# The last batch's down projection by seven products of sums, with the sums of w_out formed one stage earlier

## The chip, the cores and the metric

The kernel runs on one core of a Trainium2 chip. A core has a matrix engine (PE, with its weight loads shown as PEld), three engines for element-wise work (DVE, ACT and POOL) and a queue that issues most transfers (SP). Each engine works through its own queue in order and waits on semaphores for the others. The metric is the device time of one execution in microseconds; lower is better.

## The reference, cut to what matters

The input is q, k and v of 8 batches, 8 heads, 576 positions and 64 numbers a head, and three weights: w_a and w_b of 512 x 1536 and w_out of 1536 x 512. Each position attends to itself and the 127 before it, with a bias that grows linearly with distance, by head. The heads' results stand side by side as x, of 4608 x 512, and a feed-forward layer of two branches follows:

```python
def _moe_ref(x, w_a, w_b, w_out):
    a = x @ w_a
    b = x @ w_b
    return (a * b @ w_out).astype(np.float32)
```

The inputs and the output are fp32.

## The kernel before

**Precision.** PE multiplies fp16. Every fp32 operand is kept as two fp16 tensors, the rounded value ("hi") and the rest ("lo"), and a product of two operands is three matmuls: hi x hi, hi x lo and lo x hi. So whatever is multiplied has first to be split: a copy to fp16 on ACT (`hi`), then a subtraction on DVE (`lo`). All matmuls of the feed-forward layer have 128 x 128 weights and 288 moving columns (half a batch's 576 positions, `HT`).

**Stages.** Batch 0's attention comes first, alone. Then for each batch b an *up projection* (x times w_a and w_b, and their element-wise product, the hidden layer, of 12 blocks of 128 rows, `NF`) and a *down projection* (hidden times w_out) follow one another, and the attention of batch b + 1 is spread over them in small pieces. After batch 6's down projection there is no attention left: batch 7's up projection and down projection stand alone.

**Up projection.** `up_fast` (line 858) computes one block f by seven products of sums and differences of operands in place of eight, in seven steps of six matmuls. Two blocks run in turn as two lanes (line 912). A step's result lies in a PSUM bank `ch` or `ef` and is read by ACT (lines 866, 878 and 884) or DVE (873, 889, 894 and 901). Several steps add to the bank of an earlier step: step 3 adds to the `ch` bank that line 866 must have copied first, step 5 after line 878, step 7 after line 889. POOL multiplies at line 896. `halve` (line 833) then splits the block's hidden layer into `h`. From batch 4 on all blocks go this way. The operands, sums of x, are formed by `split_x` (line 440) with POOL subtractions (lines 451 to 461), ACT copies (437) and DVE subtractions (438), during the down projection before.

**Down projection.** `down` (line 930) computes one 128 x 288 result at a time: 36 matmuls over the 12 blocks into one bank, which ACT copies out at line 942, and a transfer at line 943. Eight such results, 288 matmuls, make a batch.

**Weights.** w_out lies in `wdn` as hi and lo for all 12 blocks. `sums_of_weights` (line 233) forms the sums of w_a and w_b that `up_fast` needs, in POOL additions (246 to 250), ACT copies (255) and DVE subtractions (256), spread over batches 1 to 3.

**What sets the order.** PE's order is written out by hand (line 1023). The order of the other engines' queues is worked out by the scheduler when the kernel is built, from readiness and priority; lines under `tc.high_priority` come first among those that are ready, and `tc.issue_after` keeps an instruction behind another of its engine. `weave` (line 954) mixes side work between the steps of a stage by its place in the program; `Pace.along` (972) does the same for attention.

**Buffers.** `vhl` (two), `qkh` and `qkl` (two each), `v`, `qk`, `pT` (one each), `t` (four) and `phl` belong to attention and are free once the last batch's attention has read them. A buffer is given to its next user when its last reader is through.

Of the kernel before, what the change touches and what calls it, by code (L numbers as in the profile page):

```python
# [11 lines left out]
F32 = mybir.dt.float32  # L12
F16 = mybir.dt.float16
# [4 lines left out]
AF = mybir.ActivationFunctionType  # L18
ALU = mybir.AluOpType
AX = mybir.AxisListType.X  # L20

B, H, S, D = 8, 8, 576, 64
DM, DF = 512, 1536
P = 128
NPAIR = H // 2
NKC = DM // P
NF = DF // P
NE = DM // P
HT = S // 2
VCOLS = 640  # L30
# [16 lines left out]
def attention_then_bilinear_ffn(ctx: ExitStack, tc: tile.TileContext, qT, kT, vP, w_a, w_b, w_out, rel, slopes2, outT):  # L47
    nc = tc.nc
    vec, act, pe, pool, sp = nc.vector, nc.scalar, nc.tensor, nc.gpsimd, nc.sync

    const = ctx.enter_context(tc.tile_pool(name="const", bufs=1))
    work = ctx.enter_context(tc.tile_pool(name="work", bufs=1))
    small = ctx.enter_context(tc.tile_pool(name="small", bufs=2))
    ps_ch = ctx.enter_context(tc.tile_pool(name="ps_ch", bufs=2, space=bass.MemoryType.PSUM))
    ps_ef = ctx.enter_context(tc.tile_pool(name="ps_ef", bufs=3, space=bass.MemoryType.PSUM))
# [177 lines left out]
    def sums_of_weights():  # L233


        spare = cycle([wup[:, f, 4:6, :, :, :].rearrange("p a c k f -> p (a c k f)").bitcast(F32).rearrange("p (s f) -> p s f", s=4) for f in range(8, NF)])

        def place():
            return next(spare) if f < 8 else work.tile([P, 4, P], F32, tag="t", name="ws32", bufs=4)

        late = []
        for f, k in [(f, k) for f in range(NF) for k in range(2)] + [(None, None)] * 1:
            if f is not None:
                a, z = place(), place()
                with tc.issue_after(last_bias[0].ins):
                    pool.tensor_tensor(out=a, in0=wup[:, f, 0:4, 0, k, :], in1=wup[:, f, 0:4, 1, k, :], op=ALU.add)
                pool.tensor_tensor(out=z[:, 0, :], in0=a[:, 3, :], in1=a[:, 2, :], op=ALU.add)
                pool.tensor_tensor(out=z[:, 2, :], in0=a[:, 0, :], in1=a[:, 3, :], op=ALU.subtract)
                pool.tensor_tensor(out=z[:, 1, :], in0=z[:, 0, :], in1=a[:, 0, :], op=ALU.subtract)
                pool.tensor_tensor(out=z[:, 3, :], in0=a[:, 1, :], in1=z[:, 1, :], op=ALU.subtract)  # L250
            late.append((f, k, z))
            if len(late) > 1:
                g, m, x = late.pop(0)
                with tc.issue_after(last_main[0].ins):
                    act.copy(wup[:, g, 3:7, 0, m, :], x)
                vec.tensor_tensor(out=wup[:, g, 3:7, 1, m, :], in0=x, in1=wup[:, g, 3:7, 0, m, :], op=ALU.subtract)  # L256
            yield
# [31 lines left out]
    def new_pT():  # L289
        return work.tile([P, 2 * NCOL // P, P], F16, tag="pT", name="pT")  # L290
# [487 lines left out]
    def new_hidden():  # L778
        return work.tile([P, 2, HT], F32, tag="rc", name="rc", bufs=3)
# [50 lines left out]
    def row():  # L830
        return work.tile([P, HT], F32, tag="row", name="row", bufs=2)

    def halve(hid, f, h, eng):
        act.copy(h[:, f, :, 0, :], hid)  # L834
        eng.tensor_tensor(out=h[:, f, :, 1, :], in0=hid, in1=h[:, f, :, 0, :], op=ALU.subtract)  # L835
# [22 lines left out]
    def up_fast(st, f, h):  # L858

        ch = ps_ch.tile([P, 512], F32, tag="ch", name="ch")[:, 0:HT]  # L860
        hid, mid = new_hidden(), row()
        x0, x1 = hid[:, 0, :], hid[:, 1, :]

        terms(ch, (f, 0), 0, True, True)
        with tc.high_priority(offset=PRIO):
            last_read[0] = last_main[0] = act.copy(x0, ch)  # L866
            first_reads[:] = first_reads[1:] + last_read
        yield

        ps = ps_ef.tile([P, 512], F32, tag="ef", name="p2")[:, 0:HT]  # L870
        terms(ps, (f, 1), 1, True, True)
        with tc.high_priority(offset=PRIO):
            vec.tensor_tensor(out=x0, in0=ps, in1=x0, op=ALU.add)  # L873
        yield

        terms(ch, (f, 4), 5, False, True)
        with tc.high_priority(offset=PRIO):
            last_read[0] = last_main[0] = act.activation(mid, ch, AF.Copy, scale=st.g)  # L878
        yield

        ps = ps_ef.tile([P, 512], F32, tag="ef", name="p7")[:, 0:HT]
        terms(ps, (f, 5), 6, True, True)
        with tc.high_priority(offset=PRIO):
            last_read[0] = last_main[0] = act.copy(x1, ps)
        yield

        terms(ch, (f, 3), 4, False, True)
        with tc.high_priority(offset=PRIO):
            vec.tensor_tensor(out=x1, in0=ch, in1=x1, op=ALU.add)
        yield  # L890

        terms(ps, (f, 2), 3, False, True)
        with tc.high_priority(offset=PRIO):
            vec.scalar_tensor_tensor(out=mid, in0=ps, scalar=st.g, in1=mid, op0=ALU.mult, op1=ALU.add)  # L894
        with tc.high_priority(offset=PRIO):
            pool.tensor_tensor(out=x0, in0=x0, in1=mid, op=ALU.mult)  # L896
        yield

        terms(ch, (f, 6), 2, False, True)
        with tc.high_priority(offset=PRIO):  # L900
            vec.scalar_tensor_tensor(out=x1, in0=x1, scalar=st.g, in1=ch, op0=ALU.mult, op1=ALU.mult)  # L901
        with tc.high_priority(offset=PRIO):
            halve(hid, f, h, vec)
        yield

    def up(st, h, plain, fast):

        for f in plain:
            yield from up_plain(st, f, h)


        lanes = [chain.from_iterable(up_fast(st, f, h) for f in fast[n::2]) for n in range(2)]
        sizes = [cycle((2, 2, 2, 1)) for _ in lanes]
        for _ in range(4 if fast else 0):
            next(lanes[0])
            yield
        for _ in range(2 if fast else 0):
            next(sizes[0])
        n = 1
        live = [True, True] if fast else []  # L920
        while any(live):
            for _ in range(next(sizes[n])):
                try:
                    next(lanes[n])
                    yield
                except StopIteration:
                    live[n] = False
            n = 1 - n

    def down(b, oi, h, order):  # L930
        started["down"] = b
        for t in range(2):
            for e in range(NE):
                ps = bank("dn_ps")
                for m, f in enumerate(order):
                    for n, (wi, hi) in enumerate(((0, 0), (0, 1), (1, 0))):
                        pe.matmul(ps[:, 0:HT], wdn[:, f, wi, e * P:(e + 1) * P], h[:, f, t, hi, :], start=(m == 0 and n == 0), stop=(m == NF - 1 and n == 2))  # L937
                    if m % 2 and m < NF - 1:
                        yield
                o = row()  # L940
                with tc.high_priority(offset=PRIO):
                    last_read[0] = last_main[0] = act.activation(o, ps[:, 0:HT], AF.Copy, scale=oi)  # L942
                act.dma_start(outT[e * P:(e + 1) * P, b * S + t * HT:b * S + (t + 1) * HT], o)
                yield

    def out_scale(st):

        oi = small.tile([P, 1], F32, tag="oi", name="oi")
        vec.tensor_scalar(out=oi, in0=st.g, scalar1=smin, scalar2=so, op0=ALU.mult, op1=ALU.mult)
        vec.tensor_scalar(out=oi, in0=oi, scalar1=st.sv, scalar2=st.sv, op0=ALU.mult, op1=ALU.mult)  # L950
        vec.reciprocal(oi, oi)
        return oi

    def weave(main, *sides):

        for n, _ in enumerate(main):
            for side, a, z, steps in sides:
                if a <= n < z:
                    for _ in range((n + 1 - a) * steps // (z - a) - (n - a) * steps // (z - a)):
                        next(side, None)  # L960

    class Pace:


        def __init__(self, steps):
            self.steps, self.at = steps, -1
# [31 lines left out]
    ways = [(every, [])] * 2 + [(every[6:], every[:6]), (every[10:], every[:10])] + [([], every)] * (B - 4)  # L998
    att = Pace(attention())
    spread = sums_of_weights()  # L1000

    quota = [((), ()), (((8, 48, 9),), ((0, 48, 4),)), (((0, 24, 3),), ((0, 48, 5),)), ((), ((0, 48, 4),))] + [((), ())] * (B - 4)

# [7 lines left out]
    def batch(b):  # L1011
        plain, fast = ways[b]
        n = 4 * len(plain) + 7 * len(fast)
        weave(att.along(up(states[b], h, plain, fast), n, NPAIR * b + 4), *((spread, *x) for x in quota[b][0]))
        weave(att.along(down(b, out_scale(states[b]), h, plain + fast), 48, NPAIR * b + 6), *((spread, *x) for x in quota[b][1]))
        if b + 1 < B:
            assert b + 1 in states

    with tc.manual_schedule(engines=SP):
        first_batch()  # L1020
# [45 lines left out]
```

## Time and profile before

| What | Value |
|---|---|
| Median of 3 runs | 1001.16 us (1000.23 to 1001.62) |
| The profiled execution's own time | 1000.39 us |
| Its span, first to last instruction | 998.6 us, 23815 instructions |
| Mean granted clock of PE | 0.988 |
| PE busy | 966.7 us, 97% of the span |
| DVE busy | 666.4 us, 67% |
| ACT busy | 633.7 us, 63% |
| POOL busy | 257.7 us, 26% |
| PE in the chain that ended last | 72% of the span |

The page divides the span into 40 slices of 25 us and shows each engine's busy tenths. The rows of the engines for the whole run:

```profile
PE   7899979999999999999999999999999999999998
PEld 5567756777777777777787777777777777877776
DVE  5979999547878566786778677666677576524530
ACT  5967669557766757767767767677666766413321
POOL 1211112113655311452226122131223022211100
```

A digit is the share of the slice in tenths, and 9 is 90% or more. The last six slices are batch 7's up and down projection, and in them DVE, ACT and POOL have less to do than elsewhere, as there is no attention beside them. An engine's busy time contains time in which an instruction has begun and is held up.

### The profile page before, as it was taken

To read this page: it belongs to the slowest core of one execution; us is meant where nothing else is said; L and a number is where in the kernel's file an instruction comes from. 1 tells how busy PE (TensorE), PEld (TensorE's weight loads), DVE (VectorE), ACT (ScalarE), POOL (GpSimd) and SP (SyncE) were. 2 spreads that over 40 slices of the span, in tenths; PEclk is the share of its full clock that TensorE was granted. 3 is DMA by queue.
4 is the path that set the end of the run, shared out by engine and by line. 5 is a ranking of instruction groups with operands and counts; after the bars stand their busy time and mean duration, and the time that the engine had idled before them with its cause. 6 is when DMAs were issued, how large, how long until landed. Compare 5 with 4: busy or idle time off the path is not lost.

```text
span 998.6 us, 23815 instructions
## 1 busy us (share of the span) xinstructions
PE 966.7 (97%) x9339; PEld 751.2 (75%) x9339; DVE 666.4 (67%) x1843; ACT 633.7 (63%) x1705; POOL 257.7 (26%) x309
## 2 busy tenths in 40 slices
PE   7899979999999999999999999999999999999998
PEld 5567756777777777777787777777777777877776
DVE  5979999547878566786778677666677576524530
ACT  5967669557766757767767767677666766413321
POOL 1211112113655311452226122131223022211100
PEclk8999979999999999999999999999999999999999
DMA  8435653474345342473533642374334532210001
GB/s 337 163 115 180 225 151 58 108 174 90 77 91 127 112 90 56 90 171 83 106 68 96 167 91 60 80 186 109 72 67 102 161 68 44 49 37 7 1 13 36
DMA packets 148432, 102.82 MB, mean 103 GB/s; under 512 B 120032, under 2 KB 128352, under 8 KB 147296
## 3 DMA queue, kind: packets, MB, share of 16 engines
q1 hardware_dynamic: 138816, 91.77, 37.7%
q10 hardware_dynamic: 9504, 9.54, 3.0%
q8 instruction: 73, 1.20, 0.5%
q14 instruction: 39, 0.32, 0.1%
HBM read 48.33 MB, written 9.44 MB: 58 GB/s over the span
## 4 chain that ended last, share of the span: by engine, by line
PE 72%; DVE 12%; ACT 6%; DMA 6%; issue 2%; SPq 1%; POOL 0%; ACTq 0%; DVEq 0%
PE ch L841 19%; PE dn_ps L937 18%; PE p L841 14%; PE up_ps L841 13%; PE x_ps L503 4%; DMA v<-in_vP 3%; PE sc_ps L380 3%; DVE phl L402 2%; PE dn_ps L817 1%; DVE xs L438 1%; DMA qk<-in_kT 1%; ACT phl L401 1%; ACT t L385 1%; DVE t L384 1%; DVE wup L256 1%
## 5 line engine op out<-in xcount | busy, mean ns | idle before, releaser
L841 PEld LDWEIGHTS <-wup 128*128 128x128 f16 x4224 | 408.3, 98 | 116.7 <-issue 10.5
L937 PE MATMUL dn_ps<-h,wdn 128*128 128x288 f16 x2016 | 254.4, 286 | 0.0
L937 PEld LDWEIGHTS <-wdn 128*128 128x128 f16 x2016 | 193.9, 98 | 51.8
L841 PE MATMUL ch<-xs,wup 128*128 128x288 f16 x1536 | 221.8, 286 | 1.2 <-ACT rc L866 0.7
L841 PE MATMUL up_ps<-xs,wup 128*128 128x288 f16 x1536 | 195.7, 287 | 2.3 <-ACT rc L788 1.5
L841 PE MATMUL p<-xs,wup 128*128 128x288 f16 x1152 | 172.6, 286 | 0.0
L896 POOL TENSOR_TENSOR rc<-rc,row 128x288 f32<-128x288 f32 x64 | 62.1, 971 | 278.0 <-DVE row L894 262.1
L385 ACT ACTIVATE t<-t,mn 128x192 f32<-128x192 f32 (+2 forms) x252 | 107.1, 427 | 25.7 <-DVE mn L384 25.5
L402 DVE SCALAR_TENSOR_TENSOR phl<-t,rin,phl 128x192 f16<-128x192 f32 (+2 forms) x252 | 106.5, 461 | 21.5 <-ACT phl L401 21.3
L834 ACT CAST h<-rc 128x576 f16<-128x576 f32 x96 | 64.1, 668 | 67.0 <-DVE rc L901 37.2
L401 ACT ACTIVATE phl<-t,rin 128x192 f16<-128x192 f32 (+2 forms) x252 | 88.7, 425 | 26.5 <-DMA pT<-phl 13.7
L835 DVE TENSOR_TENSOR h<-rc,h 128x576 f16<-128x576 f32 x90 | 69.1, 768 | 31.5 <-ACT h L834 30.7
L384 DVE CUSTOM_DVE_ANT_0 t<-sc_ps,bias,neg 128x192 f32<-128x192 f32 (+2 forms) x216 | 73.7, 389 | 9.2 <-PE sc_ps L380 9.2
L438 DVE TENSOR_TENSOR xs<-v,xs 128x576 f16<-128x576 f32 x52 | 48.3, 943 | 22.3 <-ACT xs L437 22.1
L942 ACT ACTIVATE row<-dn_ps,oi 128x288 f32<-128x288 f32 x56 | 27.7, 494 | 55.8 <-PE dn_ps L937 55.8
L878 ACT ACTIVATE row<-ch,g 128x288 f32<-128x288 f32 x64 | 31.9, 498 | 48.8 <-PE ch L841 48.8
L873 DVE TENSOR_TENSOR rc<-p,rc 128x288 f32<-128x288 f32 x64 | 29.1, 454 | 44.2 <-PE p L841 34.8
L361 POOL TENSOR_SCALAR bias<-rel_sb,ninv,sl_sb 128x192 f32<-128x192 f32 x24 | 21.4, 891 | 125.9 <-DVE mn L384 125.9
L503 PE MATMUL x_ps<-pT,vhl 128*64 128x128 f16 (+2 forms) x1176 | 44.2, 232 | 8.4 <-ACT vhl L296 5.6
L503 PEld LDWEIGHTS <-vhl 128*64 128x64 f16 x1176 | 41.6, 112 | 13.2 <-ACT vhl L296 5.9
L432 POOL TENSOR_TENSOR xq<-xq,sq 128x576 bf16<-128x576 bf16 x22 | 29.9, 1361 | 72.3 <-ACT sq L431 72.3
L901 DVE SCALAR_TENSOR_TENSOR rc<-rc,g,ch 128x288 f32<-128x288 f32 x64 | 32.6, 510 | 23.6 <-PE ch L841 23.4
(148 smaller groups left out, 1261.9 us busy)
## 6 DMA issues: line engine op xcount, KB each, us to landing
v<-in_vP SPq DMA_DIRECT2D x8, 1280.0 KB, 6.8
out<-row ACTq DMA_DIRECT2D x60, 144.0 KB, 1.8
qk<-in_qT SPq DMA_DIRECT2D x28, 288.0 KB, 4.0
qk<-in_kT SPq DMA_DIRECT2D x28, 288.0 KB, 4.5
wdn<-in_w_a SPq DMA_DIRECT2D x12, 512.0 KB, 5.1
wdn<-in_w_b SPq DMA_DIRECT2D x12, 512.0 KB, 6.0
wdn<-in_w_out SPq DMA_DIRECT2D x12, 512.0 KB, 4.3
qst<-qkh SPq DMA_DIRECT2D x24, 144.0 KB, 2.7
```

The lines of the kernel that those rows point to most:

```text
L384: vec.tensor_tensor_reduce(out=t[:, c:c + w], in0=ps[:, c:c + w], in1=o.bias[:, WIN - w:WIN], scale=-0.125 if o.b == 1 else o.neg, scalar= ...
L385: act.activation(t[:, c:c + w], t[:, c:c + w], AF.Exp, bias=o.mn[:, n:n + 1], scale=-1.0, accum_out=o.sm[:, n:n + 1])
L401: act.activation(phl[:, 0, pc:pc + w], e, AF.Copy, scale=s)
L402: vec.scalar_tensor_tensor(out=phl[:, 1, pc:pc + w], in0=e, scalar=s, in1=phl[:, 0, pc:pc + w], op0=ALU.mult, op1=ALU.subtract)
L438: vec.tensor_tensor(out=xs[:, n, 1, :, :], in0=src, in1=xs[:, n, 0, :, :], op=ALU.subtract)
L503: last = pe.matmul(xp[oc // 512][64 * h:64 * h + 64, o0:o0 + w], vt[0:rows, c:c + 64], probs(pt, rows, blocks, h), start=(n == 0 and first ...
L834: act.copy(h[:, f, :, 0, :], hid)
L835: eng.tensor_tensor(out=h[:, f, :, 1, :], in0=hid, in1=h[:, f, :, 0, :], op=ALU.subtract)
L841: pe.matmul(ps[:, 0:HT], wup[:, a[0], a[1], wi, k, :], xs[:, b, xi, k, :], start=(first and n == 0), stop=(last and n == len(ks) - 1), ski ...
L896: pool.tensor_tensor(out=x0, in0=x0, in1=mid, op=ALU.mult)
L901: vec.scalar_tensor_tensor(out=x1, in0=x1, scalar=st.g, in1=ch, op0=ALU.mult, op1=ALU.mult)
L937: pe.matmul(ps[:, 0:HT], wdn[:, f, wi, e * P:(e + 1) * P], h[:, f, t, hi, :], start=(m == 0 and n == 0), stop=(m == NF - 1 and n == 2))
```

## The change

Batch 7's hidden layer and w_out are treated as 2 x 2 blocks: two neighbouring blocks f and f + 1 of hidden rows, two halves of 288 positions, two halves of 256 output columns. Each such set of eight products of blocks is replaced by seven products of sums and differences of blocks, the scheme that `up_fast` has for the up projection. It takes three parts.

- **The sums of w_out** (`Pairs.weights`, new): for each of six pairs of blocks, two POOL additions that join hi and lo to fp32, four DVE sums of 128 x 256, then two ACT copies and two DVE subtractions of 128 x 512 that split the four sums again. The fp32 values go to `vhl`, `qkh` and `qkl`, the fp16 results to `phl`, `pT` and `t`. The work is woven into batch 6's down projection, in 14 pieces between its steps 11 and 47; what is left over runs ahead of batch 7's up projection.
- **The sums of the hidden layer** (`Pairs.hidden` and `Pairs.keep`, new): in batch 7 `up_fast` writes its blocks to the freed `v` and `qk` buffers, and `keep` stands in place of `halve`: for an even block one copy and one subtraction of half the block, for an odd one the splits and three differences, with an ACT copy of 128 x 1152 and two DVE subtractions of 128 x 576 for the four sums. They go to the part of `wup` that belongs to the even block, which is no longer needed.
- **The products** (`down_fast`, new): for each of two column blocks j and seven products, 18 matmuls over six pairs. The first two kinds are done for five of six pairs first, then for the last pair; then kinds 5, 4, 3, 2 and 6 follow for j = 0 and j = 1. Results leave in eight transfers, as before.

Batches 0 to 6 keep their `halve` and their `down`.

```diff
 def up_fast(st, f, h):
-        hid, mid = new_hidden(), row()
+        hid, mid = pairs.hidden(f) if h is None else new_hidden(), row()
...
-            halve(hid, f, h, vec)
+            if h is None:
+                pairs.keep(f)
+            else:
+                halve(hid, f, h, vec)
...
+    class Pairs:
+        def room(self):
+            big = work.tile([P, NPAIR, VCOLS], F32, tag="v", name="v_hid").rearrange("p n c -> p (n c)")
+            qk = work.tile([P, 2, S], F32, tag="qk", name="qk_hid", bufs=1).rearrange("p h s -> p (h s)")
+            self.fp32 = [x.rearrange("p (n s) -> p n s", n=4) for x in (big[:, 0:4 * HT], big[:, 4 * HT:8 * HT], qk)]
+
+        def weights(self):
+            pT = new_pT().rearrange("p a c -> p (a c)")
+            places = [phl[:, n, m:m + 1024] for n in range(2) for m in (0, 1024)] + [pT[:, m:m + 1024] for m in range(0, 4096, 1024)]
+            places += [work.tile([P, 512], F32, tag="t", name="t_ws", bufs=4).bitcast(F16) for _ in range(4)]
+            late = []
+            for i in range(NF // 2 + 1):
+                if i < NF // 2:
+                    a = [work.tile([P, 2, VCOLS], F16, tag="vhl", name="vhl_ws", bufs=2)... for _ in range(2)]
+                    zs = [work.tile([P, 2, S], F16, tag=tag, name=tag + "_ws", bufs=2)... for tag in ("qkh", "qkl")]
+                    f = 2 * i
+                    for n in range(2):
+                        pool.tensor_tensor(out=a[n], in0=wdn[:, f + n, 0, :], in1=wdn[:, f + n, 1, :], op=ALU.add)
+                    a11, a12, a21, a22 = a[0][:, 0:256], a[1][:, 0:256], a[0][:, 256:512], a[1][:, 256:512]
+                    vec.tensor_tensor(out=zs[0][:, 0, :], in0=a21, in1=a22, op=ALU.add)
+                    vec.tensor_tensor(out=zs[1][:, 0, :], in0=a11, in1=a21, op=ALU.subtract)
+                    vec.tensor_tensor(out=zs[0][:, 1, :], in0=zs[0][:, 0, :], in1=a11, op=ALU.subtract)
+                    vec.tensor_tensor(out=zs[1][:, 1, :], in0=a12, in1=zs[0][:, 1, :], op=ALU.subtract)
+                    late.append((i, zs))
+                yield
+                if i:
+                    n, zs = late.pop(0)
+                    self.sums[n] = [places[2 * n + m].rearrange("p (n w e) -> p n w e", n=2, w=2) for m in range(2)]
+                    for z, w in zip(zs, self.sums[n]):
+                        with tc.issue_after(last_main[0].ins):
+                            act.copy(w[:, :, 0, :], z)
+                        vec.tensor_tensor(out=w[:, :, 1, :], in0=z, in1=w[:, :, 0, :], op=ALU.subtract)
+                yield
+
+        def keep(self, f):
+            h, x = self.h, self.fp32[f // 2 % 3]
+            if f % 2 == 0:
+                act.copy(h[:, f, 0, 0, :], x[:, 0, :])
+                vec.tensor_tensor(out=h[:, f, 0, 1, :], in0=x[:, 0, :], in1=h[:, f, 0, 0, :], op=ALU.subtract)
+                return
+            act.copy(h[:, f, :, 0, :], x[:, 2:4, :])
+            vec.tensor_tensor(out=x[:, 0:2, :], in0=x[:, 1:4:2, :], in1=x[:, 0:2, :], op=ALU.subtract)
+            vec.tensor_tensor(out=h[:, f, :, 1, :], in0=x[:, 2:4, :], in1=h[:, f, :, 0, :], op=ALU.subtract)
+            vec.tensor_tensor(out=x[:, 3, :], in0=x[:, 3, :], in1=x[:, 0, :], op=ALU.subtract)
+            vec.tensor_tensor(out=x[:, 2, :], in0=x[:, 2, :], in1=x[:, 3, :], op=ALU.subtract)
+            tops = self.tops[f // 2] = wup[:, f - 1]...
+            act.copy(tops[:, :, 0, :], x)
+            for n in (0, 2):
+                vec.tensor_tensor(out=tops[:, n:n + 2, 1, :], in0=x[:, n:n + 2, :], in1=tops[:, n:n + 2, 0, :], op=ALU.subtract)
...
+    def down_fast(b, oi, p):
+        chs = [ps_ch.tile([P, 512], F32, tag="ch", name="dch")[:, 0:HT] for _ in range(2)]
+        p2s = [ps_ef.tile([P, 512], F32, tag="ef", name="dp2")[:, 0:HT] for _ in range(2)]
+        early = range(NF // 2 - 1)
+        for n, banks in enumerate((chs, p2s)):
+            for j in range(2):
+                p.product(banks[j], n, j, True, False, early)
+                yield
+        for n, banks in enumerate((chs, p2s)):
+            for j in range(2):
+                p.product(banks[j], n, j, False, True, (NF // 2 - 1,))
...
+        for j in range(2):
+            ch, one, two = chs[j], new_hidden(), new_hidden()
+            (x0, x1), (x2, x3) = ([x[:, n, :] for n in range(2)] for x in (one, two))
+            act.activation(x0, ch, AF.Copy, scale=oi)
+            vec.scalar_tensor_tensor(out=x0, in0=p2s[j], scalar=oi, in1=x0, op0=ALU.mult, op1=ALU.add)
+            out(j, 0, x0)
+            p.product(ch, 5, j, False, True)
+            act.activation(x2, ch, AF.Copy, scale=oi)
+            yield
...
+            p.product(ch, 6, j, False, True)
+            act.activation(x3, ch, AF.Copy, scale=oi)
+            out(j, 1, x3)
+            yield
...
 def batch(b):
+        if b == B - 1:
+            pairs.room()
+            for _ in halved:
+                pass
+            weave(up(states[b], None, plain, fast))
+            for _ in halved:
+                pass
+            for _ in down_fast(b, out_scale(states[b]), pairs):
+                pass
+            return
         weave(att.along(up(states[b], h, plain, fast), n, NPAIR * b + 4), *((spread, *x) for x in quota[b][0]))
-        weave(att.along(down(b, out_scale(states[b]), h, plain + fast), 48, NPAIR * b + 6), *((spread, *x) for x in quota[b][1]))
+        weave(att.along(down(b, out_scale(states[b]), h, plain + fast), 48, NPAIR * b + 6), *((spread, *x) for x in quota[b][1]), *[(halved, 11, 47, 14)] * (b == B - 2))
```

More of the change, by code (lines that the diff above doesn't have):

```diff
@@ L944, in down, with __init__, hidden, operands @@
                 yield
+    class Pairs:
+        def __init__(self, h):
+            self.h = h
+            self.tops, self.sums = {}, {}
+        def room(self):
[9 more added lines that the diff above has]
+                if i < NF // 2:
+                    a = [work.tile([P, 2, VCOLS], F16, tag="vhl", name="vhl_ws", bufs=2).rearrange("p h c -> p (h c)").bitcast(F32)[:, 0:DM] for _ in range(2)]
+                    zs = [work.tile([P, 2, S], F16, tag=tag, name=tag + "_ws", bufs=2).rearrange("p h s -> p (h s)").bitcast(F32)[:, 0:512].rearrange("p (n e) -> p n e", n=2) for tag in ("qkh", "qkl")]
+                    f = 2 * i
[16 more added lines that the diff above has]
+                yield
+        def hidden(self, f):
+            return self.fp32[f // 2 % 3][:, 2 * (f % 2):2 * (f % 2) + 2, :]
+        def keep(self, f):
[9 more added lines that the diff above has]
+            vec.tensor_tensor(out=x[:, 2, :], in0=x[:, 2, :], in1=x[:, 3, :], op=ALU.subtract)
+            tops = self.tops[f // 2] = wup[:, f - 1].rearrange("p n w k c -> p (n w k c)")[:, 0:8 * HT].rearrange("p (n w s) -> p n w s", n=4, w=2)
+            act.copy(tops[:, :, 0, :], x)
+            for n in (0, 2):
+                vec.tensor_tensor(out=tops[:, n:n + 2, 1, :], in0=x[:, n:n + 2, :], in1=tops[:, n:n + 2, 0, :], op=ALU.subtract)
+        def operands(self, product, i, j):
+            f, h, e = 2 * i, self.h, slice(j * P, j * P + P)
+            if product < 2:
+                return wdn[:, f + product, :, e], h[:, f + product, 0]
+            if product == 2:
+                return wdn[:, f + 1, :, 256 + j * P:256 + j * P + P], self.tops[i][:, 2]
+            k = product - 3
+            return self.sums[i][k % 2][:, k // 2, :, e], (self.tops[i][:, 0], self.tops[i][:, 1], self.tops[i][:, 3], h[:, f + 1, 1])[k]
+        def product(self, ps, product, j, first, last, some=range(NF // 2)):
+            ks = [(i, wi, hi) for i in some for wi, hi in ((0, 0), (0, 1), (1, 0))]
+            for n, (i, wi, hi) in enumerate(ks):
+                w, x = self.operands(product, i, j)
+                pe.matmul(ps, w[:, wi, :], x[:, hi, :], start=(first and n == 0), stop=(last and n == len(ks) - 1), skip_group_check=True)
@@ new lines, in down_fast, with out @@
+    def down_fast(b, oi, p):
+        started["down"] = b
+        chs = [ps_ch.tile([P, 512], F32, tag="ch", name="dch")[:, 0:HT] for _ in range(2)]
[8 more added lines that the diff above has]
+                p.product(banks[j], n, j, False, True, (NF // 2 - 1,))
+        def out(e, t, o):
+            act.dma_start(outT[e * P:(e + 1) * P, b * S + t * HT:b * S + (t + 1) * HT], o)
+        for j in range(2):
[7 more added lines that the diff above has]
+            yield
+            ps = ps_ef.tile([P, 512], F32, tag="ef", name="dp7")[:, 0:HT]
+            p.product(ps, 4, j, True, True)
+            act.activation(x1, ps, AF.Copy, scale=oi)
+            yield
+            p.product(ch, 3, j, False, True)
+            vec.scalar_tensor_tensor(out=x1, in0=ch, scalar=oi, in1=x1, op0=ALU.mult, op1=ALU.add)
+            out(j + 2, 1, x1)
+            yield
+            p.product(ps, 2, j, False, True)
+            vec.scalar_tensor_tensor(out=x2, in0=ps, scalar=oi, in1=x2, op0=ALU.mult, op1=ALU.add)
+            out(j + 2, 0, x2)
+            yield
+            p.product(ch, 6, j, False, True)
+            act.activation(x3, ch, AF.Copy, scale=oi)
+            out(j, 1, x3)
+            yield
@@ L1000, in attention_then_bilinear_ffn @@
     spread = sums_of_weights()
+    pairs = Pairs(h)
+    halved = pairs.weights()
     quota = [((), ()), (((8, 48, 9),), ((0, 48, 4),)), (((0, 24, 3),), ((0, 48, 5),)), ((), ((0, 48, 4),))] + [((), ())] * (B - 4)
@@ L1013, in batch @@
         n = 4 * len(plain) + 7 * len(fast)
+        if b == B - 1:
[8 more added lines that the diff above has]
+            return
         weave(att.along(up(states[b], h, plain, fast), n, NPAIR * b + 4), *((spread, *x) for x in quota[b][0]))
-        weave(att.along(down(b, out_scale(states[b]), h, plain + fast), 48, NPAIR * b + 6), *((spread, *x) for x in quota[b][1]))
-        if b + 1 < B:
-            assert b + 1 in states
+        weave(att.along(down(b, out_scale(states[b]), h, plain + fast), 48, NPAIR * b + 6), *((spread, *x) for x in quota[b][1]), *[(halved, 11, 47, 14)] * (b == B - 2))
+        assert b + 1 in states
     with tc.manual_schedule(engines=SP):
```

## The prediction

> **What bounds it now.** I read the busy time by stretch first, then the chain that ended last, then each engine's timeline around the last two batches. Columns of the first view: stretch, its length, then busy microseconds and instructions (in brackets) of each engine, and the granted clock.
>
> ```profile
> core 0: us, PE busy (x) PEld busy (x) DVE busy (x) ACT busy (x) POOL busy (x), PEclk, DMA share, GB/s
> ...
> 860.90:898.00 37.10, 37.10 (x335) 29.65 (x332) 10.54 (x18) 8.64 (x17) 7.53 (x5) 1.00 0.17 45
> 898.00:959.87 61.87, 61.87 (x506) 49.30 (x504) 30.20 (x58) 22.44 (x48) 8.75 (x11) 1.00 0.01 4
> 959.87:998.60 38.73, 35.45 (x290) 28.08 (x287) 1.63 (x4) 4.68 (x9) 0.80 (x1) 0.99 0.09 31
> ```
>
> The three stretches are the down projection of batch 6, then the up and the down projection of batch 7, the last. In each PE has no idle time until the last product; the rest is the last copy and its transfer. DVE, ACT and POOL are half idle. So PE sets the end, and the chain of work says the same in one piece:
>
> ```profile
> 960.03 35.29 PE dn_ps L937 x288
> ```
>
> That is 35.29 / 288 = 0.1225 us a matmul. Before it, the same view of PE's timeline gives the two moments that matter below:
>
> ```profile
> 869.08 1.54 PE L503 MATMUL x_ps<-pT,vhl 128*64 128x128 f16 x42
> 870.55 7.52 PE L937 MATMUL dn_ps<-h,wdn 128*128 128x288 f16 x60
> ...
> 899.56 0.90 PE L841 MATMUL ch<-xs,wup 128*128 128x288 f16 x6
> ```
>
> At 870.55 the last attention product has read its `vhl`; at 899.56 batch 7's third up step begins, which adds to the bank that its first step (898.00) filled.
>
> **What is removed.** Products: 7 x 6 pairs x 2 column blocks x 3 terms = 252 instead of 288. 36 x 0.1225 = **4.41 us** less on PE, all of it on the path. The eight output transfers stay eight, and the last one still follows one ACT copy, so the 3 us behind the last product stay.
>
> **What is added in batch 7, off the path.** Per pair of blocks DVE loses two subtractions of 128x576 and gains four of that shape and three of 128x288. With 0.74 us (L438's row, below) and 0.45 us (L873's) that is 4.3 - 1.5 = +2.8 us, 17 us in six pairs: 30.2 + 17 = 47 of 61.9 us. ACT gains about 1 us a pair. PE runs on beside it; results of a step are wanted two or more steps (0.735 us each) later. I take 0, with an upper bound of 0.2 us a pair (1.2 in all) where a result queues behind a burst of `keep`. For the last pair nothing is left to hide behind but PE's own early products:
>
> ```profile
> 960.46 0.80 POOL L896 TENSOR_TENSOR rc<-rc,row 128x288 f32<-128x288 f32 x1 [3.38 <-DVE row L894]
> ...
> 419.54 1.24 ACT L339 ACTIVATE qkh<-qk,own 128x1152 f16<-128x1152 f32 x1
> ```
>
> From the last POOL product's end (961.26) come two DVE passes of 0.74, two of 0.45, the 1152 wide ACT copy (1.24) and two more of 0.74: 5.1 us, so about 966.5 with the hand-overs. PE has 60 early and 12 late products of the first two kinds from 959.9 on, 8.8 us, to 968.7. Hidden by 2 us; the bound if that cover goes is a few tenths. I take 0.
>
> **What is added in batch 6's down projection.** Here is the price. For each of six pairs: two POOL additions of 128x512, four DVE operations of 128x256, two ACT copies of 128x512, two DVE subtractions of 128x512. The sums of w_a and w_b earlier in the kernel are the same kinds (durations least, median, greatest in ns):
>
> ```profile
> L246 POOL TENSOR_TENSOR ws<-wup x8: 1152/1155/1543, 413.2 to 557.1; 128x512 f32<-128x512 f16 x8
> ...
> L255 ACT CAST wup<-ws x8: 603/606/617, 428.3 to 568.1; 128x512 f16<-128x512 f32 x8
> ...
> L256 DVE TENSOR_TENSOR wup<-ws,wup x8: 681/784/1235, 429.0 to 568.7; 128x512 f16<-128x512 f32 x8
> ```
>
> ```profile
> L873 DVE TENSOR_TENSOR rc<-p,rc 128x288 f32<-128x288 f32 x64 | 29.1, 454 | 44.2 <-PE p L841 34.8
> ```
>
> The 128x256 form does not occur. It lies between L873's 0.45 and half of L256's 0.68 (0.34); from 0.68 for 512 and 0.45 for 288 I take 0.41. POOL: 12 x 1.155 = 13.9 us. DVE: 24 x 0.41 + 12 x 0.69 = 9.8 + 8.3 = 18.1 us. Each alone fits into the 27 us from 870.6 to 898. The question is whether they fit together, and what happened in that very stretch speaks against it:
>
> ```profile
> 871.33 1.41 POOL L454 TENSOR_TENSOR v<-v 128x576 f32<-128x576 f32 x1 [8.46 <-ACT v L416]
> 872.69 1.79 POOL L432 TENSOR_TENSOR xq<-xq,sq 128x576 bf16<-128x576 bf16 x1
> 875.25 1.78 POOL L456 TENSOR_TENSOR v<-v 128x576 f32<-128x576 f32 x1 [0.76 <-DVE xs L438]
> 877.11 1.41 POOL L461 TENSOR_TENSOR v<-v 128x576 f32<-128x576 f32 x1
> ```
>
> ```profile
> 857.73 0.74 DVE L438 TENSOR_TENSOR xs<-v,xs 128x576 f16<-128x576 f32 x1
> ...
> 871.80 1.54 DVE L438 TENSOR_TENSOR xs<-v,xs 128x576 f16<-128x576 f32 x1 [7.44 <-ACT xs L437]
> ```
>
> L438 takes 0.74 us alone. Begun at 871.80, while POOL worked until 872.74, it ended at 873.34: POOL's end plus 0.60. POOL's next, L432, stands at 872.69 but lasts until 874.48, which is 873.34 plus 1.14. They take turns, whole instruction by whole instruction: a DVE operation that reads two SBUF tensors and a POOL operation do not run together. [...]
>
> All the added POOL and DVE work is of these kinds, and so are the four POOL operations above (1.41 + 1.14 + 1.41 + 1.41 = 5.4 us unhindered) and five L438 (3.7). One after the other: 13.9 + 5.4 + 18.1 + 3.7 = 41.1 us; neighbours on DVE overlap by some 0.07 us, 41 times, which leaves **38.2 us**. It can begin when `vhl` is free: 870.6 + 38.2 = **908.8**, eleven microseconds into the up projection.
>
> That alone would not hurt, as the sums are read only from 968 on. But DVE, ACT and POOL run their queues in an order written when the kernel is built, and an instruction whose data are there waits behind one whose data are not. Did that order know of the turns? ACT's timeline answers:
>
> ```profile
> 877.06 0.67 ACT L437 CAST xs<-v 128x576 f16<-128x576 f32 x1 [3.18 <-POOL v L456]
> 877.64 0.49 ACT L942 ACTIVATE row<-dn_ps,oi 128x288 f32<-128x288 f32 x1
> ...
> 878.55 0.67 ACT L437 CAST xs<-v 128x576 f16<-128x576 f32 x1 [0.42 <-POOL v L461]
> ```
>
> L942 has priority over L437, and its products were done at 870.55 + 42 x 0.1225 = 875.7; yet it stands behind the L437 that waits for L456 until 877.04. Without turns L456 would have ended at 871.33 + 1.41 + 1.14 + 1.41 = 875.3, ahead of 875.7, and L461 at 876.7, behind it: exactly the order written. So the order is one that knows nothing of the turns. Without them a pair takes 2 x 1.155 + 4 x 0.35 = 3.7 us, POOL to DVE and back for the two `vhl` buffers, six pairs 22 us, and with POOL's own four 5.4: it is over at 870.6 + 27.6 = 898.2, just ahead of batch 7's first copies:
>
> ```profile
> 899.11 0.40 ACT L866 COPY rc<-ch 128x288 f32<-128x288 f32 x1 [0.41 <-PE ch L841]
> ...
> 899.74 0.46 DVE L873 TENSOR_TENSOR rc<-p,rc 128x288 f32<-128x288 f32 x1 [17.55 <-PE p L841]
> ```
>
> I therefore put the last pair's two ACT copies ahead of L866 in ACT's queue. Queued behind them is L866, and behind that PE's third step. In time: the last sums at 908.8 less the two subtractions that still follow, about 907.5; two copies of 0.6, the second to 908.3; L866 0.4; PE's third step at 908.8 instead of 899.56: a stall of **9.2 us** where PE had none. Bounds: 3.5 us (only DVE's queue is late, below) to 12.8 (0.45 for the 256 wide form: +1.0; 0.1 us lost at each of 26 hand-overs: +2.6).
>
> **The clock behind a stall.** The one such gap that the trace holds:
>
> ```profile
> 131.10:141.40 10.30, 6.03 (x57) 4.25 (x58) 10.29 (x17) 4.78 (x10) 1.61 (x1) 0.50 0.31 111
> ...
> 133.57 0.37 PE L503 MATMUL x_ps<-pT,vhl 128*64 128x128 f16 x4 [5.59 <-ACT vhl L296]
> ```
>
> PE idled 5.59 us, and the granted clock was 0.50 until 141.4; 6.03 us of work at half speed lost 3.0. There a second gap stood behind the first; behind this one PE is dense, so I take 2.5 us, bounds 0 and 10.3 / 2 = 5.1. [...]
>
> **Sum**, against the profiled execution's own 1000.39 us (span 998.6): 1000.39 - 4.41 + 9.2 + 2.5 = **1007.7 us**. The median of the runs shown lies 0.77 above that execution, within their spread; I leave the forecast on its scale.
>
> **Rivals.**
> - *The cover holds: faster.* If the order puts batch 7's copies ahead of what is late, or the sums end before about 903, PE loses less than it gains. Place: ACT's and DVE's queues at 899 to 905. It decides at a stall of 4.4 us; at none the time is 1000.39 - 4.41 = 996.0, with `keep`'s 1.2 us 997.2. For it: 27 us against 18.1 and 13.9 taken singly, and PE busy for 37.10 of 37.10 us in the same stretch. Against it: the turns above, and L942's place.
> [...]
> - *The stall without the clock:* 1005.2, part of the forecast's own range.
>
> **Chances.** Forecast 0.68 (own range 1002.5 to 1013), faster 0.17, no change 0.12, worse than 1013 0.03. The range runs from the no-change case, 999.5, to the upper bounds of stall and clock taken mostly together (12.8 + 5.1 gives 1013.9), 1013.0; it leaves out the faster rival and the worst, 0.20. A measurement of this kernel tells about 0.2% (2 us) from no change. Faster 0.19 (0.17 and a shorter DVE wait), within 0.14, slower 0.67.
>
> **What would show it.** In the changed kernel's trace: PE idle some 9 us before the third up step of batch 7, ended by L866; L866 near 908, just behind the last `places` copy; POOL additions of up to 1.8 us and DVE subtractions of up to 1.9 against each other from 871 to 909; a granted clock below 1 shortly after; then 10.3 us a pair, and 252 products in 30.9 us at the end. Wrong if L866 runs at 899 with PE dense, if DVE and POOL are through by 903, or if PE idles behind `keep` or before the tail's third kind of product.

## The result

| | before | changed |
|---|---|---|
| Median of 6 runs each, taken together | 1001.39 us | 1005.91 us (1003.65 to 1007.34) |
| Ratio to before | | 1.0056, 95% interval 1.0042 to 1.0070 |
| The profiled execution's own time | 1000.39 us | 1004.98 us |
| Its span | 998.6 us | 1003.2 us |

The change makes the kernel slower by half a per cent. One of the six runs of before took 1646.3 us, the others 998.34 to 1001.73; the ratio, from the fast runs of each kernel, does not contain it.

On the page of before, batch 7's two stages fill the last four slices, not six: they begin at 898 us, and the two slices ahead of them are mostly batch 6's down projection, where the new work goes. In the changed kernel L973 are the new additions, L975 to L978 the four sums, L986 the copies and L987 the subtractions that split them; L945 copies out a result of batch 6 and L946 issues its transfer (L942 and L943 of before).

The view of PE's waits, from batch 6's down projection to the end of the changed kernel, has one row (who waited for whom, microseconds in total, times, longest):

```profile
PE ch L841 <- ACT v_hid L866: 7.7, 1, 7.7
```

PE's timeline shows where. Columns are start, length, engine, line, tile and count, then the idle time before and who ended it.

```profile
897.58 0.90 PE L841 MATMUL ch<-xs,wup 128*128 128x288 f16 x6
898.31 0.90 PE L841 MATMUL p<-xs,wup 128*128 128x288 f16 x6
906.88 1.60 PE L841 MATMUL ch<-xs,wup 128*128 128x288 f16 x6 [7.66 <-ACT v_hid L866]
908.27 1.64 PE L841 MATMUL p<-xs,wup 128*128 128x288 f16 x6
909.71 1.16 PE L841 MATMUL ch<-xs,wup 128*128 128x288 f16 x6
910.71 0.90 PE L841 MATMUL p<-xs,wup 128*128 128x288 f16 x6
```

Two things are to be seen. The third up step of batch 7 waits 7.66 us for L866. And the three steps behind the gap start 1.39, 1.44 and 1.00 us apart where a step takes 0.735: 1.6 us more. In ACT's timeline L866 stands behind the last two copies of the sums, and these wait for DVE:

```profile
904.06 0.62 ACT L986 CAST t_ws<-qkh_ws 128x512 f16<-128x512 f32 x1 [2.99 <-DVE qkh_ws L977]
905.00 0.62 ACT L986 CAST t_ws<-qkl_ws 128x512 f16<-128x512 f32 x1 [0.32 <-DVE qkl_ws L978]
905.52 0.50 ACT L945 ACTIVATE row<-dn_ps,oi 128x288 f32<-128x288 f32 x1
906.05 0.34 ACTq L946 DMA_DIRECT2D out<-row  x1
906.43 0.40 ACT L866 COPY v_hid<-ch 128x288 f32<-128x288 f32 x1 [0.41 <-ACT row L945]
```

Why DVE is late is to be read in POOL's and DVE's timelines side by side. POOL, two additions merged in a row (its idle time of 2.3 to 2.4 us, ended by L977, is the wait for a `vhl` buffer, apart from the turns):

```profile
890.42 2.44 POOL L973 TENSOR_TENSOR vhl_ws<-wdn 128x512 f32<-128x512 f16 x2 [2.06 <-DVE oi L1073]
895.28 2.45 POOL L973 TENSOR_TENSOR vhl_ws<-wdn 128x512 f32<-128x512 f16 x2 [2.43 <-DVE qkh_ws L977]
900.04 2.43 POOL L973 TENSOR_TENSOR vhl_ws<-wdn 128x512 f32<-128x512 f16 x2 [2.30 <-DVE qkh_ws L977]
```

DVE, with the same kind of operation once behind a POOL addition and once alone:

```profile
891.78 1.36 DVE L976 TENSOR_TENSOR qkl_ws<-vhl_ws 128x256 f32<-128x256 f32 x1 [1.05 <-POOL vhl_ws L973]
...
894.27 0.41 DVE L975 TENSOR_TENSOR qkh_ws<-vhl_ws 128x256 f32<-128x256 f32 x1
...
896.65 1.36 DVE L976 TENSOR_TENSOR qkl_ws<-vhl_ws 128x256 f32<-128x256 f32 x1 [1.06 <-POOL vhl_ws L973]
```

A 128x256 operation takes 0.41 us alone. L976 begins while the second POOL addition runs and takes 1.36 us, until 0.3 us behind POOL's end (893.14 against 892.86). All six L976 took 1.31 to 1.50 us, by the view of that line:

```profile
L976 DVE TENSOR_TENSOR qkl_ws<-vhl_ws x6: 1308/1362/1496, 844.9 to 901.4; 128x256 f32<-128x256 f32 x6
```

L384, a DVE operation with one of its two inputs in PSUM (`sc_ps`, the other is `bias`), was not held up: it took 0.42 and 0.41 us at 841.96 and 842.30, alone, and the same at 843.63 and 843.98, beside the first of the new POOL additions (843.34 to 844.49).

From the end of the slow steps to the last product nothing is lost. Busy time by stretch (the columns are those of the prediction's first view), then the first and the last piece of the chain in the tail:

```profile
912.90:968.60 55.70, 55.70 (x457) 44.45 (x455) 41.65 (x80) 24.43 (x48) 8.73 (x11) 1.00 0.00 1
```

```profile
968.98 3.67 PE dch L1024 x30
...
997.64 2.22 PE dch L1024 x18
999.86 0.02 issue
999.89 0.50 ACT rc L1064
```

The 252 products run without a gap from 968.98 to 999.86, 30.9 us instead of 35.3. The account in the changed execution: 7.7 + 1.6 - 4.4, and the up projection began 0.4 us earlier (897.58 against 898.00): +4.5, against 4.59 measured.

### The profile page after: what moved, and what is told of

It is laid out like the page before. It is cut to its first block, busy times and chain, and to the rows that moved or that the text cites. A ratio compares the mean times of both kernels' runs of the same rounds, so it can differ in the third digit from the quotient of the medians.

```text
span 1003.2 us, 23846 instructions
## 1 busy us (share of the span) xinstructions
PE 963.6 (96%) x9303; PEld 748.1 (75%) x9303; DVE 711.6 (71%) x1915; ACT 645.4 (64%) x1723; POOL 273.4 (27%) x321
## 4 chain that ended last, share of the span: by engine, by line
PE 67%; DVE 17%; ACT 6%; DMA 5%; issue 3%; POOL 1%; SPq 0%; ACTq 0%; DVEq 0%; POOLq 0%
PE ch L841 19%; PE p L841 14%; PE dn_ps L940 12%; PE up_ps L841 11%; PE x_ps L503 4%; PE sc_ps L380 3%; DVE phl L402 2%; DVE xs L438 2%; PE dch L1024 2%; DMA qk<-in_kT 2%; PE dn_ps L817 1%; PE dp L1024 1%; DVE t L384 1%; DVE wup L133 1%; DVE wup L256 1%
## 5 line engine op out<-in xcount | busy, mean ns | idle before, releaser
L940 PE MATMUL dn_ps<-h,wdn 128*128 128x288 f16 x1728 | 218.9, 286 | 0.0
L940 PEld LDWEIGHTS <-wdn 128*128 128x128 f16 x1728 | 165.8, 98 | 44.7
L896 POOL TENSOR_TENSOR rc<-rc,row 128x288 f32<-128x288 f32 x52 | 52.5, 1010 | 205.4 <-DVE row L894 189.5
L834 ACT CAST h<-rc 128x576 f16<-128x576 f32 x84 | 56.1, 668 | 50.6 <-DVE rc L901 23.4
L384 DVE CUSTOM_DVE_ANT_0 t<-sc_ps,bias,neg 128x192 f32<-128x192 f32 (+2 forms) x216 | 73.7, 390 | 9.1 <-PE sc_ps L380 9.1
L835 DVE TENSOR_TENSOR h<-rc,h 128x576 f16<-128x576 f32 x78 | 60.2, 772 | 26.8 <-ACT h L834 26.3
L438 DVE TENSOR_TENSOR xs<-v,xs 128x576 f16<-128x576 f32 x52 | 48.3, 939 | 20.2 <-ACT xs L437 20.1
L385 ACT ACTIVATION_READ_ACCUMULATOR t<-t,mn 128x1 f32 x252 | 47.6, 189 | 0.0
L437 ACT CAST xs<-v 128x576 f16<-128x576 f32 x52 | 34.1, 668 | 17.4 <-POOL v L456 7.4
L380 PEld LDWEIGHTS <-qst 128*64 128x64 f16 x864 | 30.5, 110 | 16.5 <-issue 14.2
```

What stands on the lines that cost most here:

```text
L380: pe.matmul(ps[64 * e:64 * e + 64, c:c + w], o.qs[:, e, qq], ks[:, e, kk], start=not last, stop=last)
L384: vec.tensor_tensor_reduce(out=t[:, c:c + w], in0=ps[:, c:c + w], in1=o.bias[:, WIN - w:WIN], scale=-0.125 if o.b == 1 else o.neg, scalar= ...
L385: act.activation(t[:, c:c + w], t[:, c:c + w], AF.Exp, bias=o.mn[:, n:n + 1], scale=-1.0, accum_out=o.sm[:, n:n + 1])
L438: vec.tensor_tensor(out=xs[:, n, 1, :, :], in0=src, in1=xs[:, n, 0, :, :], op=ALU.subtract)
```

## The experiments

The theory: POOL operations and DVE operations that read two SBUF tensors take turns, as L976 did above (1.31 to 1.50 us instead of 0.41); the queues were ordered as if they ran side by side (this is inferred from L942's and L866's places, not read from the scheduler); so the sums end late, and the copies queued ahead of L866 hold PE up. The rivals: the mere amount of work, the rest of the change, and DVE's queue instead of ACT's. Each ratio is to before, run on the same chip. In e2_no_sums the products read w_out's own halves in place of the sums, so its output is another. The gap is that before the third up step of batch 7.

| Run | What differs from the changed kernel | Gap, us | Ratio (95% interval) |
|---|---|---|---|
| changed kernel | | 7.7 | 1.0056 (1.0042 to 1.0070) |
| e2_no_sums | sums of w_out left out | none | 0.9954 (0.9939 to 0.9969) |
| e3_sums_alone | sums formed, products of before | 7.7 | 1.0098 (1.0068 to 1.0128) |
| e1_add_on_dve | POOL additions on DVE | 2.7 | 1.0007 (0.9996 to 1.0019) |
| e7_all_on_dve | and `split_x`'s subtractions on DVE | 0.6 | 0.9966 (0.9951 to 0.9982) |
| e5_copies_behind | last pair's copies behind L866 | 3.1 | 1.0002 (0.9992 to 1.0013) |
| e6_filled | PE kept busy in the gap | 0.3 | 1.0032 (1.0019 to 1.0045) |
| e4_six_in_up | six of 14 pieces beside batch 7's up projection | none | 0.9958 (0.9946 to 0.9971) |

**Where the loss sits: one part at a time.** First the change without its sums:

```diff
         def weights(self):
+            for i in range(NF // 2):
+                self.sums[i] = [wdn[:, 2 * i + m].rearrange("p w (n e) -> p n w e", n=2) for m in range(2)]
+            return
```

> The sums of w_out are not formed; the products read w_out's own halves in their place, so the output is another. All else of the change stays: keep, seven products, 252 matmuls. Turns theory: all of the loss sits in forming the sums; PE is dense from 860 to the last product, before minus 4.4 us (ratio 0.9956, 0.9945 to 0.9967). Rival (keep's extra 2.8 us of DVE work a pair, or the chain behind the last pair, holds PE up): PE gaps of 0.2 us or more a pair or a gap before the third kind of product, ratio 0.997 to 1.000.

Then the sums without what they are for:

```diff
-            pairs.room()
             for _ in halved:
                 pass
-            weave(up(states[b], None, plain, fast))
+            weave(up(states[b], h, plain, fast))
...
-            for _ in down_fast(b, out_scale(states[b]), pairs):
+            for _ in down(b, out_scale(states[b]), h, plain + fast):
                 pass
```

> The sums are formed as in the changed kernel, but batch 7 keeps halve and the eight products of before (288 matmuls), so the sums are not used. Turns theory: the same gap of about 7.7 us before the third up step of batch 7 and 1.6 us more at half clock, nothing saved: before plus 8.5 to 9.5 us (ratio 1.0085 to 1.0095). Rival (the loss comes from the products of sums or from keep): close to before, ratio 0.999 to 1.003.

Both came out as the theory has them; the 1.0098 lies a little over the expected 1.0085 to 1.0095, which its interval contains. Without the sums the view of PE's waits is empty from 850 us on, and the ratio 0.9954 is the full saving (4.41 us are 0.0044 of before). With the sums alone the gap is the same 7.7 us although batch 7 is that of before:

```profile
PE ch L841 <- ACT rc L866: 7.7, 1, 7.7
```

So `keep` and `down_fast` cost nothing, and all of the loss comes from forming the sums.

**Turns, or amount?** The additions move from POOL to DVE, which then has more to do:

```diff
-                        pool.tensor_tensor(out=a[n], in0=wdn[:, f + n, 0, :], in1=wdn[:, f + n, 1, :], op=ALU.add)
+                        vec.tensor_tensor(out=a[n], in0=wdn[:, f + n, 0, :], in1=wdn[:, f + n, 1, :], op=ALU.add)
```

> Only the twelve 128x512 additions move from POOL to DVE; DVE gets 12 x 0.69 = 8.3 us more work in batch 6's down projection, POOL 13.9 us less. Turns theory (POOL and two-input DVE operations exclude each other, and the queues were ordered without knowing it): with no POOL additions left there is nothing to take turns with but the four old subtractions, the order holds, the first L866 of batch 7 runs near 899.5 instead of 906.4, PE idles under 1 us there, the granted clock stays 1.00, and the time is before minus 3.5 to 4.4 us (ratio 0.9955 to 0.9965). Rival (it is the mere amount of added work on DVE and ACT ahead of batch 7): DVE has more of it, so L866 and L873 are at least as late as in the changed kernel and the ratio is 1.005 or more.

Neither side was right in size: the gap fell to 2.7 us, not to under 1, the clock fell behind it, against the expectation (last section; 1.7 us), and the two together eat up the 4.4 us saved, so that the time came out like before. The rival is out, since DVE had 8.3 us more and L866 ran earlier, at 902.03. What remained are the old POOL operations, three subtractions of `split_x` and the addition of line 432. In this run's DVE timeline four operations still stand against them:

```profile
871.56 1.63 DVE L975 TENSOR_TENSOR qkh_ws<-vhl_ws 128x256 f32<-128x256 f32 x1
873.11 1.83 DVE L438 TENSOR_TENSOR xs<-v,xs 128x576 f16<-128x576 f32 x1
...
876.20 1.89 DVE L973 TENSOR_TENSOR vhl_ws<-wdn 128x512 f32<-128x512 f16 x1
878.02 1.96 DVE L438 TENSOR_TENSOR xs<-v,xs 128x576 f16<-128x576 f32 x1
```

Alone they take 0.41, 0.74, 0.68 and 0.74 us: 4.7 us lost. The next run takes the subtractions away too and gives DVE their work; the addition of line 432 stays on POOL:

```diff
-def split_x(st, plain, fast):
+def split_x(st, plain, fast, eng=pool):
...
-        pool.tensor_tensor(out=b11, in0=b12, in1=b11, op=ALU.subtract)
+        eng.tensor_tensor(out=b11, in0=b12, in1=b11, op=ALU.subtract)
...
-split_x(st, b - 1 <= 3, b - 1 >= 2)
+split_x(st, b - 1 <= 3, b - 1 >= 2, vec if b == B else pool)
```

> As the run with the additions on DVE, and batch 7's four subtractions of split_x on DVE too: but for one bf16 addition (L432) POOL has nothing beside the sums. DVE has 8.3 + 3.0 = 11.3 us more than in the changed kernel. Turns theory: the run before still lost 4.7 us in turns with those four subtractions (L975 1.63, L438 1.83, L973 1.89 and L438 1.96 instead of 0.41, 0.74, 0.68 and 0.74), which is why its gap was 2.7 us and not 0; without them the order holds, the gap before the third up step is under 1 us, the clock stays near 1.00, ratio 0.9956 to 0.9975. Rival (mere amount of DVE work ahead of batch 7): later than the run before, a gap over 2.7 us, ratio 1.001 or more.

The gap is 0.58 us and the ratio 0.9966, as PE's timeline has it:

```profile
901.91 0.90 PE L841 MATMUL ch<-xs,wup 128*128 128x288 f16 x6 [0.58 <-ACT v_hid L866]
```

DVE does 11.3 us more than in the changed kernel, and PE waits 7.1 us less. So it is not the amount of DVE work. (Part of the last step is order: L866 here stands between the last pair's two copies, 901.47 against 900.94 and 901.75.)

These two runs leave one thing mixed: with the turns they also take away that an addition lasts 1.15 us on POOL and 0.68 on DVE, and the hand-over between two engines. The rows of the changed kernel price the turns by themselves. From 870 to 906 us eleven DVE operations with two SBUF inputs are held up against POOL, together 11.2 us over the 0.41, 0.68 and 0.74 us that they take alone, more than the whole gap. An estimate says how much of it reaches the end: with the queues in their written order, these durations alone and 0.1 us for each hand-over (in the changed kernel 0.03 us from L977's end at 895.14 to L986, 0.15 from L894's end at 857.39 to L896), the sums would end near 898 us without turns and L866 would begin near 899, without a gap, whether an addition takes 1.15 us or 0.68; with turns the same reckoning gives 908 and 909 (measured: 906.3 and 906.4). No run takes away the turns alone.

**Which queue holds PE up.** In `batch`, 12 of the 14 pieces stay, and the last pair's copies and subtractions go into batch 7's up projection:

```diff
-*[(halved, 11, 47, 14)] * (b == B - 2))
+*[(halved, 11, 47, 12)] * (b == B - 2))
...
-            weave(up(states[b], None, plain, fast))
+            weave(up(states[b], None, plain, fast), (halved, 8, 40, 2))
```

> Only the last pair's two ACT copies and two DVE subtractions move: they go between steps 8 and 40 of batch 7's up projection. POOL and the four DVE sums of the last pair stay where they are, so the turns and the DVE queue up to the sums are as in the changed kernel. Theory (PE waits for L866, and L866 stands behind those two copies in ACT's queue): L866 follows the fifth pair's copies (901.1 in the changed kernel), one eviction and its transfer's issue, so about 902.0; the gap before the third up step falls from 7.7 to about 3.3 us, and L873 (behind the last sums, near 905) is wanted only at the tenth step, near 907.5: no second gap. Time: the changed kernel's minus 4.4 to 5, near before (ratio 0.9995 to 1.0015). Rival (DVE's queue, with L873 behind the last sums, is what PE waits for): no gain, ratio 1.005 or more.

L866 now follows the fifth pair's copies and one copy-out, and the gap is 3.10 us. ACT's timeline, then PE's:

```profile
898.18 0.62 ACT L986 CAST t_ws<-qkh_ws 128x512 f16<-128x512 f32 x1 [3.19 <-DVE qkh_ws L977]
...
898.70 0.61 ACT L986 CAST t_ws<-qkl_ws 128x512 f16<-128x512 f32 x1
899.22 0.49 ACT L945 ACTIVATE row<-dn_ps,oi 128x288 f32<-128x288 f32 x1
...
900.12 0.40 ACT L866 COPY v_hid<-ch 128x288 f32<-128x288 f32 x1 [0.41 <-ACT row L945]
```

```profile
900.57 0.90 PE L841 MATMUL ch<-xs,wup 128*128 128x288 f16 x6 [3.10 <-ACT v_hid L866]
```

The last sums on DVE are as late as ever (L978 begins 6.97 us behind the start of the up projection, 902.81 against 895.84, as in the changed kernel, 904.55 against 897.58), and L873 runs directly behind them, without a second gap on PE:

```profile
902.81 0.41 DVE L978 TENSOR_TENSOR qkl_ws<-vhl_ws,qkh_ws 128x256 f32<-128x256 f32 x1
903.14 0.44 DVE L873 TENSOR_TENSOR v_hid<-p,v_hid 128x288 f32<-128x288 f32 x1
```

So 4.6 us of the gap were the place of two copies in ACT's queue, as expected; the rest is the fifth pair's copies, the copy-out and the issue of its transfer, which stand there too.

**The slow steps behind the gap.** PE gets work for the time in which it idles:

```diff
+        if h is None and f == 0:
+            fill = ps_at.tile([P, 512], F32, tag="at", name="fill")
+            for _ in range(10):
+                terms(fill, (f, 0), 0, True, True)
         terms(ch, (f, 4), 5, False, True)
```

> Sixty matmuls of 288 columns (7.35 us) into a free PSUM bank that nobody reads are put into PE's order ahead of the third up step of batch 7, where PE idles 7.7 us in the changed kernel; nothing else changes in what is computed. Theory (the gap makes the granted clock fall to one half for a window of about 3.4 us, which costs 1.6 us): PE stays busy, the clock stays 1.00, the third step starts near 906.9 as before, and steps three to five take 0.735 us each instead of 1.39, 1.44 and 1.00: the changed kernel's time minus 1.6 us (ratio to before 1.0035 to 1.0045). Rival (the slow steps are late evictions or operands, not the clock): the same 1.0050 to 1.0060, and the steps stay slow.

L866 runs as late as before, at 906.05, and PE resumes at once at full speed, as its timeline has it:

```profile
898.70 7.51 PE L841 MATMUL fill<-xs,wup 128*128 128x288 f16 x60
906.50 0.90 PE L841 MATMUL ch<-xs,wup 128*128 128x288 f16 x6 [0.29 <-ACT v_hid L866]
907.23 0.90 PE L841 MATMUL p<-xs,wup 128*128 128x288 f16 x6
907.97 0.90 PE L841 MATMUL ch<-xs,wup 128*128 128x288 f16 x6
```

The steps start 0.73 us apart. In the changed kernel the granted clock fell from 1.00 to 0.50 within the gap, at 903.4, and came back at 910.2: 0.50 for the first 3.3 us behind the gap, which the expectation has as about 3.4, and 0.72 over the first six. Here it is 1.00. First the changed kernel, then this run:

```profile
906.88:912.90 6.02, 6.02 (x36) 4.19 (x36) 1.35 (x3) 1.30 (x3) 0.00 (x0) 0.72 0.07 25
```

```profile
906.00:912.90 6.90, 6.61 (x55) 5.13 (x54) 1.89 (x4) 2.50 (x6) 0.79 (x1) 1.00 0.07 24
```

The ratio, 1.0032, lies just under the expected 1.0035 to 1.0045, and its interval (up to 1.0045) touches that of the changed kernel (from 1.0042); it is the step times that show the clock's share, not the total.

**A version that keeps the saving.** Eight pieces before, six beside the up projection:

```diff
-*[(halved, 11, 47, 14)] * (b == B - 2))
+*[(halved, 11, 47, 8)] * (b == B - 2))
...
-            weave(up(states[b], None, plain, fast))
+            weave(up(states[b], None, plain, fast), (halved, 8, 70, 6))
```

> Eight of the fourteen pieces of the sums stay in batch 6's down projection, six go between steps 8 and 70 of batch 7's up projection, so their ACT copies and DVE subtractions stand behind the first up results in the queues. Turns theory: what must take turns before batch 7 shrinks from 38 us to about 27, what is left finds DVE's 15 us of idle time beside the up projection; L866 runs near 898 to 900, PE idles under 1.5 us in all, before minus 3 to 4.4 us (ratio 0.9956 to 0.997). Rival (DVE's time beside the up projection is not enough, or POOL additions hold keep and the evictions up): PE gaps spread over the up projection, ratio 0.999 to 1.004.

L866 runs at 899.22, PE waits 0.3 us in all of the last two stages, once, and the ratio is 0.9958: the whole of the 4.4 us, faster than before and than the changed kernel. POOL and DVE still take turns (an L987 of 0.68 us alone takes 1.64 at 895.89, beside a POOL addition); the late operations only no longer stand in front of what PE waits for.

## Why the prediction was right

The forecast was 1007.7 us for the profiled execution, and that execution took 1004.98; the median is 1005.91. Of the 2.7 us between, 1.5 are the stall and 0.9 the clock, both put too high; the rest is about what batch 7's up projection began earlier than before (0.4 us), which the forecast does not contain. Point by point:

- **Removed, 4.41 us.** 35.29 us of products became 30.88: right.
- **`keep` and the tail, 0.** Right: PE busy for 55.70 of 55.70 us, and the last pair's sums of the hidden layer were done at 974.8, 5.9 us after the last up step, for a product that starts at 977.6. e2_no_sums shows it by itself.
- **The turns.** Right in kind, by the 0.60 us of one L438; the eleven held-up operations show it, and e1 and e7 exclude the amount of work. The unknown 128x256 form took 0.41 us, the value that was taken.
- **The written order.** Right in what it came to: the copies stood ahead of L866, as L942's place had suggested; e5 shows that this place is worth 4.6 us.
- **The stall, 9.2 us: mis-sized.** It was 7.7. The step that was off is "it can begin when `vhl` is free: 870.6". One of the two `vhl` buffers is free long before, and the first addition and one DVE operation were done at 843 to 846 us (L976's first start above), 1.6 us of the 38.2 by their durations alone. From 870.28 to 906.3 it took 36.1 us; the other 0.5 us are not taken apart. The sums ended at 906.3, not at 908.8. In the other direction, a copy-out (L945) and the issue of its transfer stood between the last copy and L866, 0.8 us that the sum did not have.
- **The clock, 2.5 us: mis-sized.** It was 1.6: once PE resumed, the granted clock was 0.50 for 3.3 us (906.88 to 910.20) and 0.99 from there to 912.90, while 2.5 us would be 5 us at half speed.

None of the rivals came true in the changed kernel. e5 has the time of the no-change case, in which only DVE's queue is late (999.5 expected, a median of 1000.17 us in e5), but by another wait: PE stood before the third step, behind copies in ACT's queue, and L873 behind the late sums held nothing up. No run shows the term that this case rests on, a stall of 3.5 us that leaves the clock at full speed: behind a gap of 2.67 us e1 lost 1.7 us to the clock, behind one of 3.10 us e5 lost nothing (granted clock 1.00).

## What to carry to other kernels

Two engines that look half idle side by side may be one resource, as POOL and DVE were here (L976, 0.41 us alone, took 1.31 to 1.50 beside POOL): add up the time of POOL and of DVE operations with two SBUF inputs over the stretch before calling work hidden (here an estimated 38 us for 27), and check one pair of overlapping rows for turns. Side work that nobody needs soon must still not stand in the queue ahead of what the bounding engine waits for; place it behind the next stage's first copies rather than in the gap before them. Where a scheduler writes the queues, look in the trace for an instruction that waits behind a late one though its own data are there: that is where its reckoning may differ from the chip.

## What was unexpected

The granted clock does not follow the length of the gap alone. In e1_add_on_dve PE idled 2.67 us, and from 903.21 to 907.82 its four steps took 4.61 us instead of 2.94, 1.7 us more:

```profile
902.48 0.90 PE L841 MATMUL ch<-xs,wup 128*128 128x288 f16 x6 [2.67 <-ACT v_hid L866]
903.21 1.11 PE L841 MATMUL p<-xs,wup 128*128 128x288 f16 x6
904.12 1.64 PE L841 MATMUL ch<-xs,wup 128*128 128x288 f16 x6
905.56 1.64 PE L841 MATMUL p<-xs,wup 128*128 128x288 f16 x6
907.00 0.98 PE L841 MATMUL ch<-xs,wup 128*128 128x288 f16 x6
907.82 0.90 PE L841 MATMUL p<-xs,wup 128*128 128x288 f16 x6
```

That is as much as the gap of 7.66 us cost (1.6 us). In e5_copies_behind it idled 3.10 us, and the steps behind it start 0.73 us apart. The granted clock over a stretch behind each gap, first e1_add_on_dve, then e5_copies_behind:

```profile
905.00:920.00 15.00, 15.00 (x116) 11.55 (x114) 8.66 (x17) 5.16 (x11) 1.58 (x2) 0.93 0.00 1
```

```profile
902.00:910.00 8.00, 8.00 (x67) 6.38 (x66) 4.88 (x11) 2.43 (x7) 1.34 (x2) 1.00 0.01 2
```

What else it depends on, where in time the gap falls for instance, was not tried. And the start of batch 7's up projection wanders by some 4 us between profiled executions (895.84 in e5_copies_behind, 899.70 in e7_all_on_dve), which is why small differences were read from gaps and steps rather than from single times.
